# RWKV-style attention and a spatially gated block on one core: state and v of a head stacked to 128 rows from the second batch on

## The chip, the core and the metric

The kernel runs on one core of a Trainium2 chip. The metric is the device time of one execution in microseconds; for the kernel before, three runs gave a median of 352.72 us (351.6 to 352.75). One further execution was taken with the hardware profiler.

The engines are TensorE (PE in the profile; PEld is its weight loading), VectorE (DVE), ScalarE (ACT), GpSimd (POOL) and SyncE (SP), which here only issues DMA transfers. Each engine runs its own list of instructions in order and waits at semaphores.

## What is computed

Four batches, 8 heads, 768 tokens, head size 48; model width 384, inner width 1024, all float32.

```python
for t in range(S):                       # attention, state (B, H, 48, 48)
    cur = einsum('bhd,bhe->bhde', u * k[t], v[t])
    y[t] = einsum('bhd,bhde->bhe', r[t], state + cur)
    state = w[:, None] * state + einsum('bhd,bhe->bhde', k[t], v[t])
x = y as (B, S, 384)
h = maximum(x @ w_in, 0)                 # 384 -> 1024
u, v = h[..., :512], h[..., 512:]
v_n = (v - mean(v)) / sqrt(var(v) + 1e-6)
v_s = einsum('ts,bsd->btd', w_spatial, v_n) + b_spatial[None, :, None]
out = (u * v_s) @ w_out                  # 512 -> 384
```

## The kernel before

**Tiling.** Each batch is cut into 6 chunks of 128 tokens, so there are 24 chunks, numbered m. Tokens of a chunk lie in two halves of 64, z = 0 and 1, the first turned round, so that powers of the decay stay in range. The eight heads are four pairs p. For a chunk:

- `load_chunk` brings two tiles by SP's queue: `rk` (r and k with head dimensions on the partitions; 3 buffers) and `rkv` (r, k and v with tokens on the partitions; 3 buffers). v comes with each head's columns already padded with zeros to the width of a pair.
- `prep` multiplies rk by powers of the decay (on DVE and POOL for the first 7 chunks, on DVE alone after that), forms the diagonal term r * u * k summed over a head (three steps on `rkv`, a reduction to `dg`), scales k to `kn`, and writes the diagonal of the score tile `a`.
- `scores` multiplies k and r per head, 64x64, sixteen matmuls into PSUM tile `ps`.
- `products` multiplies k and v per head and half, sixteen matmuls of 64 stationary and 48 moving columns (eight in a batch's last chunk), into the other part of `ps`.
- `state` copies the masked scores into `a` (DVE), forms the state between the halves (`t`, "T1") and after the chunk (`s`), and lays each as blocks into a tile `sb` (ACT, two copies of 64x192 for each, function `block`).
- `apply` forms y transposed in PSUM tile `xp`: r times state, and scores times v. It is one group of matmuls with 32 stationary and 64 moving columns, 12 for each half that has a state and 24 for v: 48, or 36 in a batch's first chunk. Four column groups of 32 take turns.
- `fin` splits the result into a high part and a rest, tile `x`, both float32r, by a cast (ACT or DVE) and a subtraction on DVE.

The block after it works with pairs of such parts, three matmuls for each product (`mm3`: lines 556, 557, 558): `moe_v` (nine matmuls of 512 columns for a chunk), `moe_u` (nine of 384), `moe_sp` (eighteen of 384) and `moe_out` (twelve of 384). At the start `w_in`, `w_spatial` and `w_out` are turned into such pairs (`from_f64`, `split_sp`; three parts of w_in with matmuls at lines 367 to 369).

**The order.** A planner (`Plan.run`) builds the order of all five engines: every step is a task with the engines it may run on, a cost and a due time; at each step it takes, of the tasks that can start, the one that is late and due first, and books buffers. `pair`, `copy` and `relu` are steps with two possible engines. The order is then fixed; on the chip each engine runs its list.

Of the kernel before, what the change touches and what calls it, by code (L numbers as in the profile page):

```python
# [37 lines left out]
BIAS = 3  # L38
MOST_IN, MOST_OUT = 2, 1


class Task:
    def __init__(self, ways, lag, nominal, nbytes):
        self.ways, self.lag, self.nominal, self.nbytes = ways, lag, nominal, nbytes
        self.cost = min(w[1] for w in ways)
        self.before, self.after, self.bufs = set(), set(), []
        self.due = self.end = self.most = None
# [20 lines left out]
class Plan:  # L68
# [11 lines left out]
    def add(self, ways, r=(), w=(), lag=0.1, nominal=None, nbytes=0):  # L80
        t = Task(ways, lag, nominal, nbytes)
# [34 lines left out]

    CV = ("cv", "ws")
# [10 lines left out]

    def run(self):
        self.dues()  # L130
        left = {t: len(t.before) for t in self.tasks}
# [4 lines left out]
        while ready:  # L136
            best = {}
            for t in ready:
# [4 lines left out]
                if t.nbytes and len(landed) >= self.LANES:  # L143
                    can = max(can, landed[-self.LANES])
                end, e, at = min((max(can, free.get(e, 1.0)) + c + (BIAS if e == "DVE" else 0), e, max(can, free.get(e, 1.0)))
                                 for e, c, *_ in t.ways)
                late = at <= free.get(e, 1.0) + 0.02
                key = (0, t.due, t.place) if late else (1, at, t.due, t.place)
                if e not in best or key < best[e][0]:
                    best[e] = (key, at, t)  # L150
            if not best:
                raise ValueError(f"no slot for any of {len(ready)} ready tasks")
            _, at, t, e = min(((x[0], x[1], x[2], e) for e, x in best.items()), key=lambda x: (x[1], x[2].due))
# [31 lines left out]
            emit()  # L185
# [4 lines left out]
def fused_kernel(ctx, tc, rkT, rkvN, wT, uB, w_in, w_sp, b_sp, w_out, out):  # L190
# [4 lines left out]
    EARLY, STATS = 7, 1  # L195
# [3 lines left out]
    SLOTS = dict(rk=3, rkv=3, vn=6, gt=5, u=8, vs=4, g=2, ob=2, pm=4, ps=1, xp=1, x=2, s=2, t1=1, dg=2, q=2)  # L199
# [42 lines left out]
    def load(key, shape, dtype, src, nbytes, view=None, due=None):  # L242
# [3 lines left out]
        plan.add([("SP", 0.45, f, False)], (), [key], lag=0, nbytes=nbytes).most = due  # L246
# [11 lines left out]
    atiles = [const.tile([P, 2, 2, 2, HC], F32, name=f"a{n}") for n in range(2)]  # L258
    sblk = [const.tile([P, NP, 2 * D], F32, name=f"sb{n}") for n in range(2)]
# [10 lines left out]
    TMP = ("vs", "tmp")  # L270
# [4 lines left out]
    def sync(dst, src, key, nbytes, due=None):  # L275
        plan.add([("SP", 0.45, lambda: nc.sync.dma_start(out=dst, in_=src), False)], (), [key], lag=0,
                 nbytes=nbytes).most = due

    def setup():
# [36 lines left out]
        for n in range(2):  # L316
            pool(0, lambda n=n: nc.gpsimd.memset(sblk[n], 0.0), (), [("B", n)], cost=0.45)
# [20 lines left out]
    def load_chunk(m):  # L338
        b, c = divmod(m, NC)
        load(("rk", m), [P, 2, NP, C], F32, rkT[b, c], P * 2 * NP * C * 4)  # L340
        load(("rkv", m), [P, ROW], F32, rkvN[b, c], P * ROW * 4)
# [59 lines left out]
    def split_sp(j):  # L401
        K = ("gt", ("sp", j))
        for t in range(2):
# [3 lines left out]
            if (j, t) in SUM_SP:  # L407
# [6 lines left out]
                act(TH, lambda o=o, PS=PS: nc.scalar.copy(ws_l[:, j, o], T[PS][:, 0:TH]), [PS], [L])  # L414
# [6 lines left out]
    def prep(m):  # L421
        RK, RV, DG, A = ("rk", m), ("rkv", m), ("dg", m), ("A", m % 2)
        a = atiles[m % 2]
# [3 lines left out]
        if m < EARLY:  # L427
            pool(512, lambda: nc.gpsimd.tensor_tensor(out=rk()[:, 1], in0=rk()[:, 1], in1=tt, op=ALU.mult),
                 [RK, *TT], [k_], cost=1.1)
# [7 lines left out]
        pool(DM, lambda: nc.gpsimd.tensor_tensor(out=n_(), in0=n_(), in1=k0(), op=ALU.mult), [RV], [rn])  # L437
# [22 lines left out]
    def products(m):  # L460
        PS, RV = ("ps", m), ("rkv", m)

        def f():
            ps, rkv = tile_of(PS, [P, 2, 512]), T[RV]
            kn, v = rkv[:, OK:OK + DM + 16], rkv[:, OV:ROW].rearrange("s (z p e) -> s z p e", z=2, p=NP)
            for p2, z, s0, t0, j, b in QUAD:
                if z == 1 and m % NC == NC - 1:
                    continue
                hs, p, o = slice(64 * (j ^ b), 64 * (j ^ b) + 64), 2 * b + p2, 256 + (2 * z + p2) * D
                kc = (4 * b + 2 * p2 + z) * D  # L470
                nc.tensor.matmul(ps[64 * j:64 * j + 64, b, o:o + D], kn[hs, kc:kc + 64],  # L471
                                 v[hs, z, p, j * D:(j + 1) * D], start=True, stop=True, skip_group_check=True)

        pe(0.6 if m % NC < NC - 1 else 0.37, f, [RV + ("kn",), RV], [PS + ("k",)], nominal=(2 * m, 2))

    def block(dst, src):
        d4 = dst.rearrange("p (b q) e -> p b q e", b=2)
        nc.scalar.copy(d4[0:64, :, :, 0:D], src[0:64])
        nc.scalar.copy(d4[64:P, :, :, D:2 * D], src[64:P])

    def state(m):
        c, PS, S0, S1, T1 = m % NC, ("ps", m), ("s", m - 1), ("s", m), ("t1", m)
        part = lambda z: T[PS][:, :, 256 + z * 2 * D:256 + (z + 1) * 2 * D].rearrange("p b (q e) -> p b q e", q=2)
        sh = [P, 2, 2, D]
        dve(512, lambda: nc.vector.copy_predicated(  # L485
            out=atiles[m % 2].rearrange("s b q z t -> s (b q) (z t)"),
            mask=mask_u.rearrange("s z t -> s (z t)").unsqueeze(1).to_broadcast([P, 4, P]),
            data=T[PS][:, :, 0:256].rearrange("s b (q c) -> s b q c", q=2)),
            [PS + ("s",), ("c", "mask"), ("A", m % 2)], [("A", m % 2)], cost=0.63)
        k_ = PS + ("k",)  # L490
        if c == 0:
            act(0, lambda: block(sblk[1], part(0)), [k_], [("B", 1)], cost=0.62)
            dve(192, lambda: nc.vector.tensor_copy(out=tile_of(T1, sh), in_=part(0)), [k_], [T1])
        else:
            act(0, lambda: block(sblk[0], T[S0]), [S0], [("B", 0)], cost=0.72)
# [337 lines left out]
```

## Time and profile before

| | |
|---|---|
| runs shown, median | 352.72 us (351.6, 352.75, 352.72) |
| profiled execution | 352.11 us, span 350.4 us |
| busy in the span: PE, DVE, ACT, POOL | 329.4, 171.2, 148.6, 225.3 us |
| chain that ended last, PE's share | 88% |
| `xp`, all matmuls of apply, PE busy | 38.15 us |
| granted clock | 1.000 |

The span runs from the first to the last instruction; the execution's own time lies 1.7 us above it. An engine's busy time counts overlapping instructions once. In lists of instructions, "idle" is the time in which the engine stood still just before one, with the engine or the transfer that ended the wait behind an arrow. A float32 matmul leaves two records, so counts in the trace are twice those in the code.

### The profile page before, as it was taken

To read this page: it belongs to the slowest core of one execution; us is meant where nothing else is said; L and a number is where in the kernel's file an instruction comes from. 1 tells how busy PE (TensorE), PEld (TensorE's weight loads), DVE (VectorE), ACT (ScalarE), POOL (GpSimd) and SP (SyncE) were. 2 spreads that over 40 slices of the span, in tenths; PEclk is the share of its full clock that TensorE was granted. 3 is DMA by queue.
4 is the path that set the end of the run, shared out by engine and by line. 5 is a ranking of instruction groups with operands and counts; after the bars stand their busy time and mean duration, and the time that the engine had idled before them with its cause. 6 is when DMAs were issued, how large, how long until landed. Compare 5 with 4: busy or idle time off the path is not lost.

```text
span 350.4 us, 11537 instructions
## 1 busy us (share of the span) xinstructions
PE 329.4 (94%) x5092; PEld 302.1 (86%) x5092; DVE 171.2 (49%) x353; ACT 148.6 (42%) x334; POOL 225.3 (64%) x215
## 2 busy tenths in 40 slices
PE   2876999899999999999999999999999999999994
PEld 1454678799999899999999899999999899999993
DVE  5598964878634555554233664454233343011030
ACT  4237867772333384641323374640323363611121
POOL 4888989999858765587855767486855240436310
PEclk9999999999999999999999999999999999999999
DMA  7999457762061344442153144342050000010101
GB/s 236 421 408 341 160 177 249 250 227 89 0 199 44 134 153 153 146 129 101 22 199 115 40 152 153 144 137 96 19 203 2 2 2 2 22 47 0 45 24 67
DMA packets 13153, 44.78 MB, mean 128 GB/s; under 512 B 1584, under 2 KB 4784, under 8 KB 13104
## 3 DMA queue, kind: packets, MB, share of 16 engines
q1 hardware_dynamic: 13104, 44.05, 35.4%
q8 instruction: 40, 0.66, 0.8%
q14 instruction: 9, 0.07, 0.1%
HBM read 39.32 MB, written 4.72 MB: 126 GB/s over the span
## 4 chain that ended last, share of the span: by engine, by line
PE 88%; DVE 6%; DMA 2%; issue 2%; ACT 1%; SPq 0%; DVEq 0%; ACTq 0%
PE pm L556 24%; PE pm L557 23%; PE pm L558 23%; PE xp L516 9%; PE ps L455 4%; PE ps L471 3%; DMA vn<-w_in 1%; PE pm L367 1%; DVE a L485 1%; DVE pm L355 1%; DVE vn L357 1%; DVE pm L359 1%; DVE rk L430 1%; DMA out<-ob 1%; DVE wi_l L378 1%
## 5 line engine op out<-in xcount | busy, mean ns | idle before, releaser
L556 PE MATMUL pm<-ws_h,vn 128*128 128x384 f32 x192 | 65.2, 340 | 0.0
L558 PE MATMUL pm<-ws_h,vn 128*128 128x384 f32 x192 | 64.7, 337 | 0.0
L557 PE MATMUL pm<-ws_l,vn 128*128 128x384 f32 x192 | 64.5, 336 | 0.0
L682 DVE TENSOR_TENSOR g<-pm,bb 128x384 f32<-128x384 f32 x32 | 17.8, 556 | 66.6 <-PE pm L558 62.7
L437 POOL TENSOR_TENSOR rkv<-rkv 128x384 f32<-128x384 f32 x24 | 26.3, 1096 | 37.2 <-DMA rkv<-rkvN 37.2
L229 POOL TENSOR_TENSOR vn<-vs,vn 128x512 fp32r<-128x512 f32 x24 | 32.6, 1378 | 27.2 <-ACT vn L233 14.8
L233 ACT CAST gt<-g 128x384 fp32r<-128x384 f32 x32 | 16.4, 514 | 72.6 <-POOL g L229 66.4
L229 POOL TENSOR_TENSOR g<-g,u 128x384 f32<-128x384 f32 x30 | 31.4, 1047 | 19.1 <-DVE g L682 19.1
L434 DVE TENSOR_TENSOR rk<-rk,tt 128x1024 f32<-128x1024 f32 x17 | 29.5, 1734 | 25.9 <-DMA rk<-rkT 25.9
L229 POOL TENSOR_TENSOR gt<-g,gt 128x384 fp32r<-128x384 f32 x30 | 30.5, 1016 | 15.0 <-ACT gt L233 15.0
L556 PEld LDWEIGHTS pm<-ws_h,vn 128*128 128x128 f32 x192 | 36.0, 188 | 0.3
L557 PEld LDWEIGHTS pm<-ws_l,vn 128*128 128x128 f32 x192 | 36.1, 188 | 0.0
L558 PEld LDWEIGHTS pm<-ws_h,vn 128*128 128x128 f32 x192 | 36.0, 188 | 0.0
L556 PE MATMUL pm<-wo_h,gt 128*128 128x384 f32 x96 | 32.9, 342 | 0.0
L556 PE MATMUL pm<-x,wi_h 128*128 128x384 f32 x93 | 32.5, 349 | 0.0
L558 PE MATMUL pm<-wo_h,gt 128*128 128x384 f32 x96 | 32.4, 338 | 0.0
L557 PE MATMUL pm<-wo_l,gt 128*128 128x384 f32 x96 | 32.4, 338 | 0.0
L557 PE MATMUL pm<-x,wi_h 128*128 128x384 f32 x93 | 31.4, 338 | 0.9 <-issue 0.9
L442 POOL TENSOR_TENSOR a<-diag,dg 128x512 f32<-128x512 f32 x24 | 26.1, 1086 | 8.2 <-PE xp L516 4.9
L558 PE MATMUL pm<-x,wi_l 128*128 128x384 f32 x93 | 31.3, 337 | 0.0
L485 DVE COPY_PREDICATED a<-mask,ps 128x512 f32<-128x512 uint32 x24 | 18.0, 751 | 25.8 <-PE ps L471 22.5
L441 POOL TENSOR_TENSOR rkv<-rkv,tn 128x384 f32<-128x384 f32 x24 | 30.2, 1260 | 0.0
(119 smaller groups left out, 701.4 us busy)
## 6 DMA issues: line engine op xcount, KB each, us to landing
rkv<-rkvN SPq DMA_DIRECT2D x24, 776.0 KB, 4.6
rk<-rkT SPq DMA_DIRECT2D x24, 512.0 KB, 6.0
out<-ob SPq DMA_DIRECT2D x24, 192.0 KB, 1.9
vn<-w_in SPq DMA_DIRECT2D x6, 512.0 KB, 10.2
gt<-w_sp SPq DMA_DIRECT2D x6, 384.0 KB, 10.5
gt<-w_out SPq DMA_DIRECT2D x4, 384.0 KB, 3.8
bb<-b_sp SPq DMA_DIRECT2D x1, 384.0 KB, 9.3
ub<-uB SPq DMA_DIRECT2D x1, 192.0 KB, 7.3
```

The lines of the kernel that those rows point to most:

```text
L229: plan.add([(e, cost[e], lambda e=e: engine[e].tensor_tensor(**f()), True) for e in ways.split()], r, w)
L233: emit = dict(DVE=lambda: nc.vector.tensor_copy(**f()), ACT=lambda: nc.scalar.copy(f()["out"], f()["in_"]))
L434: dve(1024, lambda: nc.vector.tensor_tensor(out=rk(), in0=rk(), in1=tt.unsqueeze(1).to_broadcast([P, 2, NP, C]), op=ALU.mult), [RK, *TT], ...
L437: pool(DM, lambda: nc.gpsimd.tensor_tensor(out=n_(), in0=n_(), in1=k0(), op=ALU.mult), [RV], [rn])
L441: pool(DM, lambda: nc.gpsimd.tensor_tensor(out=k0(), in0=k0(), in1=tn_f, op=ALU.mult), [RV, rn, *TN], [kn])
L442: pool(512, lambda: nc.gpsimd.tensor_tensor(out=a.rearrange("s b q z t -> s (b q z) t"), in0=diag.unsqueeze(1).to_broadcast([P, H, HC]), i ...
L485: dve(512, lambda: nc.vector.copy_predicated(out=atiles[m % 2].rearrange("s b q z t -> s (b q) (z t)"), mask=mask_u.rearrange("s z t -> s ...
L516: nc.tensor.matmul(xp[32 * g:32 * g + 32, z, jt * HC:(jt + 1) * HC], lhsT, rhs, start=(z, g) not in began, stop=True, skip_group_check=Tru ...
L556: nc.tensor.matmul(o, lh, rh, start=first, stop=False)
L557: nc.tensor.matmul(o, lh, rl, start=False, stop=False)
L558: nc.tensor.matmul(o, ll, rh, start=False, stop=last)
L682: dve(384, lambda: nc.vector.tensor_tensor(out=g(), in0=T[PM][:, 0:TH], in1=bb[:, ts_], op=ALU.add), [PM, ("c", "bb")], [G])
```

## The change

From the second batch on (chunk 6, `FIRST_CHUNKS`), the state of a head and its v share a stationary operand: v takes the 64 rows of the head's half, the state 48 of the other 64 rows, in the tile `rkv` itself, where `v` now comes with 64 columns for each head, half and pair. Apply is then 8 groups of four matmuls, 32 in all, in first chunks too. The moving operand is a new tile `A` (2 buffers) with scores and r stacked in the same way. It is filled by `move`: four copies of r (64x256) and two of `a` (64x512) for a chunk, each a DMA on SP's queue, an ACT copy or a DVE copy, as the planner picks. The state goes into `rkv` by four ACT copies of 48x96 in place of two of 64x192. In the first six chunks apply keeps its 48 or 36 matmuls.

`products` takes 48 stationary columns in place of 64 in all chunks; the rows of PSUM between are set to zero once. The PSUM tile `ps` is fixed. `rk` has 2 buffers in place of 3; `a` is one buffer that is written whole (it was two, set to zero at the start). The loads of `rkv` are 1536 columns in the first six chunks and 1792 later, where they were 1552.

The planner gets biases by engine and by step (`LEAN`, `BIAS`, `LATE`), three steps of `prep` may go to DVE, and five seeds shake due times and biases of a share of the tasks.

```diff
+ROW_E, ROW = OV + 2 * NP * 2 * D, OV + 2 * 2 * NP * HC
+FIRST_CHUNKS = 6
-BIAS = 3
+LEAN = 4.0
+CALM, LATE = 80.0, dict(DVE=1.0, SP=1.0)
+SEEDS = (200055, 200068, 200448, 200760, 200881)
+BIAS = dict(DVE=3.0, ACT=3.5)
...
+    def shake(self):
+        for seed in SEEDS:
+            rnd = random.Random(seed)
+            share, size = rnd.choice((0.01, 0.03, 0.1, 0.3)), rnd.choice((1.0, 3.0, 8.0))
+            for t in self.tasks:
+                if rnd.random() < share:
+                    t.due += rnd.uniform(-size, size)
+                    for w in t.ways:
+                        w.lean += rnd.uniform(-size, size)
...
-    SLOTS = dict(rk=3, rkv=3, vn=6, ...
+    SLOTS = dict(rk=2, rkv=3, a=1, A=2, vn=6, ...
...
+        if m >= EC:
+            move(RK + ("r",), ("A", m), "r", [(64 * (1 - t), t, slice(2 * b, 2 * b + 2), 64 * (t ^ b))
+                                              for b in range(2) for t in range(2)],
+                 lambda p, h: rk()[h:h + 64, 0, p])
+
+    def move(src, dst, part, places, source):
+        for o, t, p, h in places:
+            n = (p.stop - p.start) * C
+            out = lambda o=o, t=t, p=p: tile_of(dst, [P, 2, NP, C])[o:o + 64, t, p]
+            plan.add([("SP", 0.45, lambda ...: nc.sync.dma_start(out=out(), in_=source(p, h)), False, 64 * n * 4),
+                      ("ACT", (n + 220) / 1200, lambda ...: nc.scalar.copy(out(), source(p, h))),
+                      ("DVE", n / 960 + 0.1, lambda ...: nc.vector.tensor_copy(out=out(), in_=source(p, h)),
+                       True, 0, LEAN)],
+                     [src], [dst + ((part, t, p.start),)], lag=0.1)
...
-                nc.tensor.matmul(ps[64 * j:64 * j + 64, b, o:o + D], kn[hs, kc:kc + 64],
-                                 v[hs, z, p, j * D:(j + 1) * D], start=True, stop=True, skip_group_check=True)
+                nc.tensor.matmul(ps[64 * j:64 * j + D, b, o:o + D], kn[hs, kc:kc + D],
+                                 ve[hs, h, z, p, slice(0, D) if m < EC else slice(16 * h, 16 * h + D)],
+                                 start=True, stop=True, skip_group_check=True)
...
+        for b in range(2):
+            for j in range(2):
+                h = j ^ b
+                o = 64 * (1 - h)
+                nc.scalar.copy(sv[o:o + D, h, z, 2 * b:2 * b + 2, 16 * h:16 * h + D], src[64 * j:64 * j + D, b])
...
+            sv = T[RV][:, OV:ROW].rearrange("s (h z p e) -> s h z p e", h=2, z=2, p=NP)
+            right = T["A", m]
             for z, s0, t0 in SUBS:
...
+                for j, h in ((0, 0), (1, 0), (1, 1), (2, 1)):
+                    for p in range(NP):
+                        mm(z, j, p, sv[:, h, z, p, 32 * (j - h):32 * (j - h) + 32], right[:, h, p, t0:t0 + 64])
```

The order moves with it. On PE, before, the scores, products and apply of chunk 2 stand together, behind the apply of chunk 1 and one matmul of the first moe_v:

```order
L516 MATMUL xp<-a_82,rkv 32x64 x24
L578 MATMUL pm<-wi_l,x 128x512
L455 MATMUL ps<-rk 64x64 x16
L471 MATMUL ps<-rkv 64x48 x16
L516 MATMUL xp<-rk,sb_83 32x64 x12
L516 MATMUL xp<-rk,sb_84 32x64 x12
L516 MATMUL xp<-a_81,rkv 32x64 x24
L556 MATMUL pm<-wi_h,x 128x512
```

The same place on PE now, from the end of chunk 0's moe_v (L659) on; L584 is apply, L523 products, L504 scores:

```order
L659 MATMUL pm<-wi_l,x 128x512 x3
L584 MATMUL xp<-rk,A 32x64 x24
L584 MATMUL xp<-a,rkv 32x64 x24
L523 MATMUL ps<-rkv 48x48 x16
L504 MATMUL ps<-rk 64x64 x16
L637 MATMUL pm<-wi_h,x 128x512
L638 MATMUL pm<-wi_l,x 128x512
L639 MATMUL pm<-wi_h,x 128x512
```

Nine matmuls of the second moe_v, of which the last three rows are the first three, now stand between the scores and the apply of chunk 2. A little earlier, the third conversion of w_in (L400 to L402, L367 to L369 before) has moved ahead of the first projection matmuls.

On ACT, at the first chunk of the second batch, before (L478 and L479 lay the state into `sb`):

```order
L594 ACTIVATE vs,q<-pm 128x512
L233 CAST x<-xp 128x2x3x64
L596 ACTIVATE q<-q 128x1
L478 COPY sb_84<-ps 64x4x48
L479 COPY sb_84<-ps 64x4x48
L597 ACTIVATE pm,q<-vs,q 128x512
```

And the same place on ACT now; L545 lays a state into `rkv`, L490 moves scores into `A`:

```order
L675 ACTIVATE vs,q<-pm 128x512
L677 ACTIVATE q<-q 128x1
L678 ACTIVATE pm,q<-vs,q 128x512
L545 COPY rkv<-ps 48x2x48 x4
L490 COPY A<-a 64x512 x2
L545 COPY rkv<-s 48x2x48 x4
```

The cast of x has gone to DVE, and ten copies stand where two did; the four moves of r for this chunk are on SP's queue.

On SP's queue, the loads for chunks 5 to 7, before:

```order
L245 DMA rkv_570<-rkvN 128x1552
L245 DMA rk_574<-rkT 128x1024
L245 DMA rkv_710<-rkvN 128x1552
L245 DMA rk_730<-rkT 128x1024
L245 DMA rkv_858<-rkvN 128x1552
L245 DMA rk_862<-rkT 128x1024
```

And now, from the rk of chunk 6 (885) to that of chunk 8 (1055):

```order
L277 DMA rk_885<-rkT 128x1024
L277 DMA rkv_896<-rkvL 128x1792
L489 DMA A_986<-rk_885 64x256 x4
L277 DMA rk_1013<-rkT 128x1024
L277 DMA rkv_1034<-rkvL 128x1792
L277 DMA rk_1055<-rkT 128x1024
```

Moves of r (L489) stand between the loads and wait for the multiply of `rk`; later in the list two moves of `a` stand there as well.

More of the change, by code (lines that the diff above doesn't have):

```diff
@@ L142, in run @@
                 can = max([1.0] + [b.end for b in t.before] + [min(self.slots[k[0]])[0] for k in takes])
[L143 to L146, printed above, removed]
+                found = None
+                for way in t.ways:
+                    e = way.engine
+                    at = max(can, free.get(e, 1.0))
+                    if way.nbytes and len(landed) >= self.LANES:
+                        at = max(at, landed[-self.LANES])
+                    end = (self.landing(line, at, way.nbytes) if way.nbytes else at + way.cost) + (way.lean if t.due < CALM else LATE.get(e, 0.0))
+                    if found is None or end < found[0]:
+                        found = (end, e, at, way)
+                _, e, at, way = found
                 late = at <= free.get(e, 1.0) + 0.02
@@ L157, in run @@
                 s.remove(min(s))
-            _, cost, emit, two = next(w for w in t.ways if w[0] == e)
-            if two and e == "DVE":
+            cost = way.cost
+            if way.two and e == "DVE":
                 cost += sum(max(0.0, min(y, at + cost) - max(x, at)) for x, y in shared[-3:])
-            if two and e == "POOL":
+            if way.two and e == "POOL":
                 shared.append((at, at + cost))
@@ L184, in run, with fused_kernel @@
                     ready.append(a)
-            emit()
+            way.emit()
         assert all(t.end is not None for t in self.tasks)
 @with_exitstack
-def fused_kernel(ctx, tc, rkT, rkvN, wT, uB, w_in, w_sp, b_sp, w_out, out):
+def fused_kernel(ctx, tc, rkT, rkvE, rkvL, wT, uB, w_in, w_sp, b_sp, w_out, out):
     nc = tc.nc
@@ L340, in load_chunk @@
         load(("rk", m), [P, 2, NP, C], F32, rkT[b, c], P * 2 * NP * C * 4)
[L341 removed]
+        n, src = (ROW_E, rkvE[m]) if m < EC else (ROW, rkvL[m - EC])
+        load(("rkv", m), [P, ROW], F32, src, P * n * 4, lambda t: t[:, 0:n])
     EYE, NEG = ("c", "eye"), ("c", "neg")
@@ L490, in state @@
+            [PS + ("s",), ("c", "mask"), ("a", m)], [("a", m)], cost=0.63)
+        if m >= EC:
+            move(("a", m), ("A", m), "a", [(64 * h, h, slice(0, NP), 64 * h) for h in range(2)],
+                 lambda p, h: T["a", m][h:h + 64].rearrange("s b q z t -> s (b q) (z t)"))
         k_ = PS + ("k",)
         if c == 0:
-            act(0, lambda: block(sblk[1], part(0)), [k_], [("B", 1)], cost=0.62)
+            act(0, lambda: block(m, 1, part(0)), [k_, RV], [B1], cost=0.62 if m < EC else 1.05)
@@ L739, in fused_kernel @@
         convert_in(k)
-    for n in range(2):
-        pool(0, lambda n=n: nc.gpsimd.memset(atiles[n], 0.0), (), [("A", n)], cost=0.52)
     for j in range(NS):
```

208 lines of the change are left out of this document (119 added, 89 removed).

## The prediction

> **What bounds the kernel now.** I read the page's busy times and chain first, then the busy time by stretches of the span, then the timeline of PE, DVE and ACT up to 64 us.
>
> ```profile
> PE 329.4 (94%) x5092; PEld 302.1 (86%) x5092; DVE 171.2 (49%) x353; ACT 148.6 (42%) x334; POOL 225.3 (64%) x215
> PE 88%; DVE 6%; DMA 2%; issue 2%; ACT 1%; SPq 0%; DVEq 0%; ACTq 0%
> ```
>
> ```profile
> 0.00:9.66 9.66, 1.79 (x32) 1.50 (x32) 6.09 (x13) 4.05 (x9) 3.95 (x18) 1.00 0.77 255
> 9.66:17.00 7.34, 6.84 (x72) 3.79 (x72) 3.69 (x6) 2.16 (x5) 7.18 (x8) 1.00 1.02 421
> 17.00:27.45 10.45, 7.82 (x174) 4.89 (x174) 9.94 (x20) 3.97 (x10) 8.51 (x9) 1.00 1.03 409
> 27.45:35.00 7.55, 5.01 (x232) 3.98 (x232) 6.32 (x14) 6.22 (x17) 6.61 (x7) 1.00 0.88 327
> 35.00:49.06 14.06, 12.69 (x260) 9.87 (x261) 12.14 (x31) 9.67 (x28) 12.76 (x14) 1.00 0.56 197
> 49.06:62.00 12.94, 12.09 (x337) 10.16 (x336) 6.78 (x12) 9.86 (x24) 12.94 (x12) 1.00 0.63 204
> 62.00:345.90 283.90, 283.12 (x3988) 267.95 (x3988) 126.22 (x264) 112.23 (x245) 173.34 (x153) 1.00 0.27 93
> 345.90:350.40 4.50, 0.00 (x0) 0.00 (x0) 0.00 (x0) 0.48 (x1) 0.00 (x0) 0.98 0.34 124
> ```
>
> The columns behind the length are PE, PEld, DVE, ACT, POOL, granted clock, DMA share and GB/s. There are two regimes. From 62 to 346 us PE works 283.12 of 283.90 us, so each microsecond of PE work removed there leaves the span, while DVE (126) and ACT (112) have more than half of the stretch free. Before 62 us PE idles, and from 17 to 27.45 us DVE is the full engine, 9.94 of 10.45 us. What the change does to the two regimes has to be worked out apart.
>
> **Term 1, apply.** A float32 matmul is recorded twice, so x96 is the 48 matmuls of a chunk with an incoming state, and x72 the 36 of a batch's first chunk.
>
> ```profile
> 131.77 1.48 PE xp L516 x96
> 142.88 1.14 PE xp L516 x72
> ```
>
> Twelve matmuls are 0.34 us: 28.3 ns each, and 0.12 us that doesn't go with the count. The 32 of the new form, same shapes (32 columns stationary, 64 moving), come to 1.03 us. Fifteen chunks with state go from 1.48 to 1.03 (6.75 us), three first chunks from 1.14 to 1.03 (0.33): -7.1 us. If all of the time went with the count they would take 0.99 and the gain be 7.8; less than 7.1 needs a larger fixed part than these rows have. The first six chunks keep their 252 matmuls.
>
> **Term 2, k x v with 48 stationary columns in place of 64.** No row has 48 of them. The nearest:
>
> ```profile
> 52.90 0.69 PE L455 MATMUL ps<-rk 64*64 64x64 f32 x32
> 53.41 0.40 PE L471 MATMUL ps<-rkv 64*64 64x48 f32 x16
> 53.74 0.44 PE L556 MATMUL pm<-x,wi_h 128*128 128x384 f32 x1
> 59.57 0.63 PE L471 MATMUL ps<-rkv 64*64 64x48 f32 x32
> 60.13 0.44 PE L556 MATMUL pm<-x,wi_h 128*128 128x384 f32 x1
> L471 PE MATMUL ps<-rkv 64*64 64x48 f32 x704 | 14.6, 217 | 0.7 <-DVE a L485 0.4 <-issue 0.3
> L471 PEld LDWEIGHTS ps<-rkv 64*64 64x64 f32 x704 | 12.7, 135 | 1.1 <-DVE a L485 0.7 <-issue 0.4
> L516 PEld LDWEIGHTS xp<-a,rkv 128*32 128x32 f32 x1152 | 18.3, 110 | 1.8 <-issue 1.4 <-DVE a L485 0.5
> ```
>
> From start to next start, 8 matmuls take 0.33 us and 16 take 0.56: 28.8 ns each, as much as apply's 28.3, although 48 columns move here and 64 there. So the moving side doesn't set it. Either the 64 stationary columns do (a load is 135 ns at 64 columns and 110 at 32), and 48 would save a quarter, 7.2 ns on 352 matmuls, 2.5 us; or about 28 ns is a floor, and nothing is saved. Nothing in the rows makes fewer columns dearer. I take 0.8, nearer the floor, since apply with half the stationary columns is no quicker. The Trainium skill, "TensorE: Matmul & The Clock Gate", section "Back-to-back issue gap", lists 1 to 64 moving columns at one price, an issue floor; the trace agrees that 48 and 64 cost the same (28.8 and 28.3 ns). By that rule alone this term would be 0, and the sum 0.8 us smaller.
>
> **Term 3, the start.** Where PE waits in the first 50 us:
>
> ```profile
> 19.95 0.50 PE L578 MATMUL pm<-wi_h,x 128*128 128x512 f32 x1 [0.90 <-ACT x L233]
> 20.86 0.51 PE L578 MATMUL pm<-wi_h,x 128*128 128x512 f32 x1 [0.41 <-DVE x L550]
> 27.08 0.85 PE L516 MATMUL xp<-rk,sb 128*32 128x64 f32 x21 [0.69 <-ACT sb L478]
> 29.84 0.27 PE L516 MATMUL xp<-a,rkv 128*32 128x64 f32 x2 [1.19 <-issue]
> 30.47 0.69 PE L455 MATMUL ps<-rk 64*64 64x64 f32 x32
> 33.22 0.85 PE L516 MATMUL xp<-rk,sb 128*32 128x64 f32 x21 [1.13 <-ACT sb L478]
> ...
> 55.42 0.39 PE L556 MATMUL pm<-wi_h,x 128*128 128x512 f32 x1
> 57.58 0.88 PE L516 MATMUL xp<-rk,sb 128*32 128x64 f32 x48
> 61.96 0.45 PE L557 MATMUL pm<-x,wi_h 128*128 128x384 f32 x1 [0.85 <-issue]
> ```
>
> The stretches from 17 to 62 us hold 7.4 us of idle PE (their length less PE's time), 1.19 and 0.85 of it "issue", which I count on no order to remove. The new order puts chunk 1's nine projection matmuls (2.16 us by the rows at 55.42 and 57.58) between the scores and apply of chunk 2, where 1.13 us was lost, and the third conversion's matmuls between apply and projection of chunk 0, where 0.90 + 0.41 was lost: 2.4 us covered. Of the other 2.9 us, in smaller waits such as the 0.69, I take a third, 0.9. Against that, the list of DVE up to the last w_in conversion grows by one memset, one rkv x ub, four casts of x and one of w_sp, less one multiply of rk: about 3.0 us on an engine with 3.7 us free from 17 to 49 us, where a cast before lay on ACT. I put 0.3 of it on PE's path. Two buffers of rk instead of three make chunk 2's load wait for apply 0, which ends near 19 us:
>
> ```profile
> rk<-rkT SPq DMA_DIRECT2D x24, 512.0 KB, 6.0
> gt<-w_sp SPq DMA_DIRECT2D x6, 384.0 KB, 10.5
> L428 POOL TENSOR_TENSOR rk<-rk,tt 128x512 f32<-128x512 f32 x7 | 9.0, 1286 | 0.0
> ```
>
> It lands between 25 and 29.5 us (6.0, or 10.5 behind the w_sp loads now ahead of it), plus the multiply 26.3 to 30.8; scores 2 stood at 30.47, so nothing is charged. Sum of the start: -2.4 - 0.9 + 0.3 = -3.0. Ends: -5.4 if all idle but the issue stalls goes, +0.6 if DVE's 3.0 us come wholly through and only the 2.4 are won.
>
> **Term 4, the new copies.** For 18 chunks there are 108 moves into A: 70 on ACT, 13 on DVE, 25 on SP's queue, and eight small state copies per chunk on ACT where four stood. Nearest prices:
>
> ```profile
> L478 ACT COPY sb<-t 64x192 f32<-64x192 f32 x20 | 7.0, 351 | 16.7 <-DVE t L496 16.7
> L233 ACT CAST vn<-vs 128x512 fp32r<-128x512 f32 x24 | 13.6, 613 | 0.0
> L500 DVE TENSOR_TENSOR ps<-ps,t 128x192 f32<-128x192 f32 x20 | 7.2, 359 | 0.1
> L493 DVE COPY t<-ps 128x192 f32<-128x192 f32 x4 | 1.4, 356 | 0.8 <-ACT sb L479 0.8
> L485 DVE COPY_PREDICATED a<-mask,ps 128x512 f32<-128x512 uint32 x24 | 18.0, 751 | 25.8 <-PE ps L471 22.5 <-ACT sb L479 2.2 <-PE ps L455 1.1
> ```
>
> A move of a at 0.61, one of r at about 0.45, a state copy at most 0.35: under 3.5 us of ACT per chunk of some 11 us (131.77 to 142.88 above), with ACT at 40%. PE work between scores and apply of a chunk covers them, except in one place: chunk 6, where only eighteen projection matmuls stand between products and apply, 3.8 us (1.68 and 2.16, by the starts at 53.74, 55.42 and 57.58). The chain in that gap is two DVE operations of 0.36, the predicated copy 0.75, two moves of a at 0.61 on ACT: 2.7 us, 3.3 if the four state copies delay ACT. It fits with handoffs to spare for little; I take +0.5 for this and other waits, ends 0 and +2.
>
> **Sum.** -7.1 - 0.8 - 3.0 + 0.5 = -10.4. The profiled execution took 352.11 us (span 350.4, 1.7 around it), so 341.7; the median shown, 352.72, is 0.6 above it, so 342.3. The last 4.5 us keep their instructions.
>
> **Rivals.**
> A. The start gives nothing: DVE, full there, pays for the casts, and scores 2 waits for rk. For it speaks 9.94 of 10.45; against it that the covered waits have DVE's or ACT's work on their far side, which now runs under matmuls. 352.7 - 7.1 - 0.8 + 0.5 = 345.3, up to 347.4 with the +2 of term 4.
> B. The start gives all, and 48 columns their quarter: 352.7 - 7.1 - 2.5 - 5.4 = 337.7 with no waits later; half-way from the forecast to it is 340. DVE's fullness speaks against the whole of it, the equal 28 ns against the quarter.
> C. Slower. SP's queue is in order, and moves of r and a wait in it for DVE's multiply and predicated copy; the next rk and rkv loads stand behind them, with one buffer of rk fewer.
>
> ```profile
> rkv<-rkvN SPq DMA_DIRECT2D x24, 776.0 KB, 4.6
> L434 DVE TENSOR_TENSOR rk<-rk,tt 128x1024 f32<-128x1024 f32 x17 | 29.5, 1734 | 25.9 <-DMA rk<-rkT 25.9
> L437 POOL TENSOR_TENSOR rkv<-rkv 128x384 f32<-128x384 f32 x24 | 26.3, 1096 | 37.2 <-DMA rkv<-rkvN 37.2
> ```
>
> DVE and POOL already wait for these loads (25.9 and 37.2 us in all) without PE noticing, and rkv grows by 15%. A load held past the chunk's cover costs PE 1:1. It decides at 0.58 us a chunk (10.4 / 18: no change) and is slower by over 0.5% from 0.68; at 1.0 us a chunk the time is 352.7 - 10.4 + 18 = 360. Against it: load 6.0 and multiply 1.73 are 7.7 us of an 11 us period, and only 25 of 108 moves are on SP.
>
> **Chances and range.** Forecast (339.5 to 344.5) 0.56, A 0.21, B 0.14, C 0.09. The range 338 to 347.8 holds the forecast, all of A and most of B; the forecast's own range is 339.5 to 344.5. About 0.5%, 1.8 us, is what this measurement can tell from no change. Faster: forecast, A and B, 0.90, and a little of C; no change, C near 0.58 us a chunk, 0.03; slower 0.07.
>
> **What would show it.** Term 1: xp groups of 64 records taking 1.03 us. Term 2: k x v starts 28.8 ns apart, or 21.6. Term 3: PE idle from 17 us to the steady stretch down from 7.4 to about 4.4 us, no wait of scores 2 on rk. Term 4: PE waits under 1 us before apply of chunk 6, and none later. The prediction is wrong if PE waits on ACT's moves or on loads in each chunk, or if DVE's stretch before 45 us gets longer than the waits it saves.

## The result and the profile after

| | before | after |
|---|---|---|
| median, runs beside each other | 352.58 us (4 runs) | 339.89 us (4 runs, 339.43 to 341.45) |
| ratio, with its 95% interval | | 0.9654 [0.9617, 0.9690] |
| profiled execution, span | 352.11, 350.4 us | 341.45, 339.7 us |
| busy: PE, DVE, ACT, POOL | 329.4, 171.2, 148.6, 225.3 | 319.3, 213.5, 176.2, 209.8 |

By the ratio the changed kernel is 12.2 us faster (0.0346 of 352.58); the medians differ by 12.7. Ratios, here and below, compare mean times and leave out executions that took over 1.5% longer than the fastest of the same kernel, while medians are over all. The forecast was 342.3, and 338 to 347.8 as a range. The two profiled executions differ by 10.7 us, and that is what the traces can be asked about. The page of after, its busy times and the shares of its chain:

```profile
PE 319.3 (94%) x4588; PEld 291.9 (86%) x4588; DVE 213.5 (63%) x417; ACT 176.2 (52%) x438; POOL 209.8 (62%) x195
PE 83%; DMA 6%; POOL 4%; DVE 3%; issue 2%; SPq 1%; ACT 0%; DVEq 0%; ACTq 0%
```

PE lost 504 records (16 matmuls in each of 15 chunks and 4 in each of three first chunks, recorded twice) and 10.1 us of busy time; DVE and ACT gained 42 and 28 us. The chain now crosses transfers (6%, 2% before) and POOL (4%), a sign that there is less spare room round PE than there was.

Where the 10.7 us lie is read from the busy times by stretches, cut at 17 us by the clock and after that at the same work in both traces: at the start of apply 6 (the first stacked one), at the end of apply 23, at PE's end. Columns: stretch, length, then PE, PEld, DVE, ACT and POOL busy, granted clock, DMA share, GB/s. Before:

```profile
0.00:17.00 17.00, 8.63 (x104) 5.28 (x104) 9.77 (x18) 6.22 (x14) 11.13 (x25) 1.00 0.88 327
17.00:65.17 48.17, 40.78 (x1018) 31.41 (x1022) 38.03 (x79) 32.79 (x84) 43.99 (x42) 1.00 0.74 269
65.17:290.98 225.81, 225.50 (x3670) 211.69 (x3669) 113.40 (x233) 94.64 (x207) 154.24 (x135) 1.00 0.31 108
290.98:345.42 54.44, 54.44 (x310) 53.74 (x306) 9.96 (x24) 14.48 (x29) 15.94 (x15) 1.00 0.06 23
345.42:350.40 4.98, 0.00 (x1) 0.00 (x0) 0.00 (x0) 0.51 (x2) 0.00 (x0) 0.98 0.32 118
```

After:

```profile
0.00:17.00 17.00, 8.81 (x176) 5.79 (x176) 13.33 (x25) 7.17 (x15) 10.55 (x22) 1.00 0.87 328
17.00:62.70 45.70, 38.93 (x942) 30.20 (x942) 38.48 (x81) 27.19 (x71) 40.11 (x38) 0.96 0.69 249
62.70:282.20 219.50, 217.58 (x3166) 202.55 (x3165) 148.60 (x285) 127.95 (x325) 143.99 (x122) 1.00 0.41 137
282.20:336.22 54.02, 54.02 (x307) 53.35 (x306) 13.05 (x28) 13.39 (x27) 15.16 (x14) 1.00 0.09 30
336.22:339.70 3.48, 0.00 (x0) 0.00 (x0) 0.00 (x0) 0.48 (x1) 0.00 (x0) 0.97 0.16 57
```

Up to apply 6: 2.5 us won. From there to the end of apply 23: 6.3. To PE's end: 0.4. Behind PE: 1.5. In the long stretch PE's busy time fell by 7.9 (225.50 to 217.58), and its idle time rose from 0.3 to 1.9.

The rows of PE that answer to the terms: k x v of a last and of a full chunk, each with the next row, and apply 6.

```profile
50.51 0.36 PE L523 MATMUL ps<-rkv 64*48 64x48 f32 x16
50.79 0.44 PE L637 MATMUL pm<-x,wi_h 128*128 128x384 f32 x1
58.39 0.54 PE L523 MATMUL ps<-rkv 64*48 64x48 f32 x32
58.86 0.44 PE L637 MATMUL pm<-x,wi_h 128*128 128x384 f32 x1
62.71 1.13 PE L584 MATMUL xp<-A,rkv 128*32 128x64 f32 x64
63.76 0.44 PE L637 MATMUL pm<-x,wi_h 128*128 128x384 f32 x1
```

Start to start, eight k x v matmuls take 0.28 us and sixteen 0.47: 23.75 ns each, where 28.8 stood (the rows are given to 0.01 us, so this is good to some 2 ns). Apply takes 1.05 from start to start. And PE's waits of over 0.75 us from 20 us on, with what ended them:

```profile
22.71 0.57 PE L523 MATMUL ps<-rkv 64*48 64x48 f32 x32 [1.96 <-DVE a L552]
28.64 0.98 PE L504 MATMUL ps<-rk 64*64 64x64 f32 x32 [1.28 <-POOL rk L462]
...
53.57 0.47 PE L637 MATMUL pm<-wi_h,x 128*128 128x512 f32 x1 [0.95 <-DVE x L265]
66.38 0.69 PE L504 MATMUL ps<-rk 64*64 64x64 f32 x32 [0.76 <-DVE rk L468]
75.58 1.15 PE L584 MATMUL xp<-A,rkv 128*32 128x64 f32 x64 [1.16 <-issue]
```

The last two are new in kind. The scores of chunk 7 wait for DVE's multiply of rk, and DVE had itself stood 2.80 us for the load of that rk:

```profile
65.10 1.23 DVE L468 TENSOR_TENSOR rk<-rk,tt 128x1024 f32<-128x1024 f32 x1 [2.80 <-DMA rk<-rkT]
```

Apply 7 waits for something that the profile does not name. After 76 us PE doesn't wait for as long as 0.3 us in one place.

### The profile page after: what moved, and what is told of

Its sections match the earlier page's. It is cut to its first block, busy times and chain, and to the rows that moved or that the text cites. A ratio compares the mean times of both kernels' runs of the same rounds, so it can differ in the third digit from the quotient of the medians.

```text
span 339.7 us, 10768 instructions
## 1 busy us (share of the span) xinstructions
PE 319.3 (94%) x4588; PEld 291.9 (86%) x4588; DVE 213.5 (63%) x417; ACT 176.2 (52%) x438; POOL 209.8 (62%) x195
## 4 chain that ended last, share of the span: by engine, by line
PE 83%; DMA 6%; POOL 4%; DVE 3%; issue 2%; SPq 1%; ACT 0%; DVEq 0%; ACTq 0%
PE pm L637 25%; PE pm L639 23%; PE pm L638 23%; PE xp L584 6%; PE ps L504 4%; DMA rk<-rkT 3%; DMA vn<-w_in 3%; PE ps L523 2%; POOL rkv L260 1%; POOL rk L462 1%; SPq L277 1%; POOL vn L260 1%; POOL a L260 1%; DVE pm L388 1%; PE pm L659 0%
## 5 line engine op out<-in xcount | busy, mean ns | idle before, releaser
L260 POOL TENSOR_TENSOR a<-diag,dg 128x512 f32<-128x512 f32 x24 | 27.0, 1126 | 38.5 <-ACT A L490 15.2
L265 ACT CAST gt<-g 128x384 fp32r<-128x384 f32 x28 | 14.2, 513 | 60.7 <-POOL g L260 51.3
L260 POOL TENSOR_TENSOR gt<-g,gt 128x384 fp32r<-128x384 f32 x28 | 29.8, 1067 | 17.1 <-ACT gt L265 16.2
L260 POOL TENSOR_TENSOR g<-g,u 128x384 f32<-128x384 f32 x27 | 29.5, 1093 | 15.3 <-DVE g L763 15.1
L468 DVE TENSOR_TENSOR rk<-rk,tt 128x1024 f32<-128x1024 f32 x17 | 28.9, 1699 | 11.2 <-DMA rk<-rkT 9.8
L260 POOL TENSOR_TENSOR vn<-vs,vn 128x512 fp32r<-128x512 f32 x16 | 22.9, 1444 | 21.1 <-ACT vn L265 21.1
L260 POOL TENSOR_TENSOR rkv<-rkv,tn 128x384 f32<-128x384 f32 x24 | 31.2, 1298 | 1.5 <-DVE rkv L260 1.5
L260 POOL TENSOR_TENSOR rkv<-rkv 128x384 f32<-128x384 f32 x21 | 22.0, 1049 | 15.1 <-DMA rkv<-rkvL 9.2
L637 PE MATMUL pm<-wi_h,x 128*128 128x512 f32 x69 | 28.0, 406 | 0.9 <-DVE x L265 0.9
## 6 DMA issues: line engine op xcount, KB each, us to landing
vn<-w_in SPq DMA_DIRECT2D x6, 512.0 KB, 10.1
gt<-w_sp SPq DMA_DIRECT2D x6, 384.0 KB, 10.2
```

Source lines behind the costliest of these rows:

```text
L265: emit = dict(DVE=lambda: nc.vector.tensor_copy(**f()), ACT=lambda: nc.scalar.copy(f()["out"], f()["in_"]))
L468: dve(1024, lambda: nc.vector.tensor_tensor(out=rk(), in0=rk(), in1=tt.unsqueeze(1).to_broadcast([P, 2, NP, C]), op=ALU.mult), [RK, *TT], ...
L637: nc.tensor.matmul(o, lh, rh, start=first, stop=False)
```

## Experiments

Two things were open: how much each part of the change is worth by itself, and whether the order, which the forecast took as given and priced only by its waits, is itself what the time hangs on. Times below are medians; ratios are against the kernel before, run beside.

**Stationary columns alone.** The kernel before with 48 stationary columns in k x v, a fixed `ps` tile and its zeroes; nothing else.

```diff
-                nc.tensor.matmul(ps[64 * j:64 * j + 64, b, o:o + D], kn[hs, kc:kc + 64],
+                nc.tensor.matmul(ps[64 * j:64 * j + D, b, o:o + D], kn[hs, kc:kc + D],
```

> The kernel before, with k x v on 48 stationary columns in place of 64 and nothing else (PSUM tile fixed, its spare rows set to zero once; order of all engines kept). In the changed kernel a set of 16 products went from 0.56 to 0.47 us, start to next start, a set of 8 from 0.33 to 0.28. Theory, the stationary columns set the time: 20 x 0.09 + 4 x 0.05 = 2.0 us off, 350.6 us. Rival, a floor of 28 ns per matmul, the shorter sets being due to what stands behind them: no change, 352.6.

350.52 us, ratio 0.9951 [0.9936, 0.9966]: 1.7 us faster. Fewer stationary columns make these matmuls quicker, so 28 ns was no floor: the trace's own slope, (28.8 - 23.75) ns on 16 or 8 matmuls of 24 chunks, is 20 x 0.08 + 4 x 0.04, some 1.8 us. The Trainium skill, "TensorE: Matmul & The Clock Gate", section "Back-to-back issue gap", lists one price for 1 to 64 moving columns, and by that alone this would be 0; the same section says that weight loading and matmul set the spacing together, which is the half that the runs bear out (a load is 122 ns at 48 columns, 135 at 64).

**No seeds.** The changed kernel with `SEEDS = ()`: same instructions for PE, another order.

> The changed kernel with an empty list of seeds, so due times aren't shaken; stacking, 48 columns, biases and buffers stay. PE's work is the same. Theory, the gain is PE's work (7.1 apply + 2.0 products) and the rest, about 3.6 us, is the order of the start and the end, half of it from the seeds: 341.5 us. Rival 1, the seeds carry all that goes beyond PE's work: 343.5 or more. Rival 2, they do nothing on the chip: 339.9.

352.19 us, ratio 0.9983 [0.9956, 1.0009], from 349.24 to 357.61 in twelve runs. The number lies in rival 1's open range, "343.5 or more", but rival 1 kept the gain of PE's work, and that is gone too: without the five seeds nothing is left of the gain that this measurement can tell from no change. PE has the same matmuls in it as the kernel that takes 339.9. In the two profiles PE's busy time is 321.3 us here and 319.3 there, and its idle time in the span 27.2 and 20.4.

**No seeds and no stacking.** All 24 chunks in the first form.

```diff
-FIRST_CHUNKS = 6
+FIRST_CHUNKS = 24
-SEEDS = (200055, 200068, 200448, 200760, 200881)
+SEEDS = ()
```

> The changed kernel without stacking (FIRST_CHUNKS = 24) and without seeds: apply keeps 48 or 36 matmuls in all chunks, no moves into A. To be held against the run without seeds. Theory, apply's count is worth 15 x 0.45 + 3 x 0.11 = 7.1 us and its copies are hidden: 7 us above the run without seeds, about 348.5. Rival, the copies and waits for loads take a part back in the changed kernel: only 4 to 5 us above it, with fewer waits of PE here than there.

353.59 us, ratio 1.0044 [1.0017, 1.0070]. Between this and the run above stacking is worth 1.4 us by the medians and 2.1 by the ratios, not 7.1. In the stretch from apply 6 to apply 23 the two profiles, this one first, say why:

```profile
65.20:291.80 226.60, 223.61 (x3670) 209.46 (x3669) 141.40 (x278) 82.27 (x184) 125.90 (x117) 1.00 0.32 112
65.00:289.70 224.70, 218.94 (x3166) 204.12 (x3165) 154.01 (x292) 122.78 (x309) 143.93 (x125) 0.99 0.39 129
```

PE's work falls by 4.7 us, at a lower clock, and its idle time rises from 3.0 to 5.8, while ACT has 40 us more to do.

**Other seeds, and the planner as it was.** First `SEEDS = (1, 2, 3, 4, 5)`, then the stacked kernel with the settings of before:

```diff
-LEAN = 4.0
-CALM, LATE = 80.0, dict(DVE=1.0, SP=1.0)
-SEEDS = (200055, 200068, 200448, 200760, 200881)
-BIAS = dict(DVE=3.0, ACT=3.5)
+LEAN = 99.0
+CALM, LATE = 1e9, {}
+SEEDS = ()
+BIAS = dict(DVE=3.0)
```

> SEEDS = (1, 2, 3, 4, 5) in place of the five in the change: a shake that nobody chose by its time. Theory (it is this one order that is quick, the shake as such gives nothing): 349 to 356, like the orders without seeds (352.2 and 353.6). Rival (any spreading of the due times takes the waits away): 339 to 345.

> Stacked chunks and 48 columns as in the change, but the planner's settings of before: no seeds, LEAN 99 (so that DVE isn't offered the new ways), the bias of 3 for DVE alone, CALM never reached. Theory (without a chosen order the copies' waits take back most of apply's 7 us): 349 to 354. Rival (the new leans and biases are what hurts without the seeds, the old ones keep the 7 + 2 us): 343 to 346.

357.82 us, ratio 1.0156 [1.0130, 1.0181], and 360.34 us, ratio 1.0250 [1.0210, 1.0289]. A shake as such gives nothing, and both came out slower than their theories had it. With the old settings the stacked kernel, 9 us lighter on PE, is 8.4 us slower than before. Much of the cost lies in one place, the stretch from 60 to 90 us, where the first stacked chunks, the conversion of w_out and the loads meet. Old settings, then the changed kernel:

```profile
60.00:90.00 30.00, 21.31 (x413) 17.95 (x412) 20.75 (x41) 23.10 (x64) 22.16 (x18) 0.84 0.35 118
60.00:90.00 30.00, 28.08 (x385) 26.07 (x385) 23.80 (x47) 16.67 (x45) 27.90 (x25) 1.00 0.76 257
```

PE stands for 8.7 us of the 30 and the mean granted clock is 0.84; in the changed kernel it stands for 1.9 at the full clock.

**Which part of the order.** The same draws of the same five seeds, but put to use only on tasks due before 62 us, or only on the others:

```diff
+        plain = {t: t.due for t in self.tasks}
...
+                    on = float(plain[t] < 62.0)
-                    t.due += rnd.uniform(-size, size)
+                    t.due += on * rnd.uniform(-size, size)
...
-                        w.lean += rnd.uniform(-size, size)
+                        w.lean += on * rnd.uniform(-size, size)
```

> The five seeds draw the same numbers as in the changed kernel, but only the due times and leans of tasks due before 62 us are shaken. The no-seeds run, 352.2, and the changed kernel, 339.9, differ by 12.3 us; in the profiled executions 2.3 of it lie before apply of chunk 6, 5.2 between there and the end of apply 23, 1.3 behind the last matmul. Theory (the stretches add up, each stretch keeps what its own order gives): the start's 2.3 are won, 349.5 to 350.5. Rival (the start's order sets how far the copies are ahead of PE from then on, so that the late shake only follows): 342 to 345. Rival (an order holds as a whole only): 352.

> The same draws, but only tasks due at 62 us or later are shaken; PE's list then differs from the changed kernel's by about 100 lines, nearly all in the start. Theory (stretches add up): the steady part and the tail come out as in the changed kernel, the start as without seeds: 341.5 to 345, with a start of apply 6 at 65 us and from there to the end of apply 23 219.5 to 221 us. Rival (the start decides): 349 to 352, with 223 us or more in that stretch.

Early alone: 344.80 us, ratio 0.9801 [0.9759, 0.9842], which is in the first rival's range. Late alone (`>=`): 347.92 us, ratio 0.9880 [0.9827, 0.9934], between its theory and its rival. The two gains against the run without seeds are 7.4 and 4.3 us by the medians and 6.4 and 3.6 by the ratios; both shakes together give 12.3 and 11.6. With intervals of 1 to 2 us on each, the time adds up by parts, but not by the parts in which I had put it. Long stretch and tail, early alone:

```profile
61.80:283.40 221.60, 217.21 (x3166) 202.47 (x3165) 154.31 (x295) 126.29 (x318) 142.58 (x122) 1.00 0.39 135
337.44:342.30 4.86, 0.00 (x0) 0.00 (x0) 0.00 (x0) 0.51 (x2) 0.00 (x0) 0.94 0.34 121
```

and late alone:

```profile
65.30:289.20 223.90, 219.21 (x3166) 204.31 (x3165) 148.00 (x286) 125.80 (x318) 143.55 (x121) 0.98 0.39 131
343.20:346.50 3.30, 0.00 (x0) 0.00 (x0) 0.00 (x0) 0.48 (x1) 0.00 (x0) 1.00 0.16 60
```

Against 65.0, 224.7 and 4.8 without seeds, the early shake wins 3.2 us before apply 6 and 3.1 behind it, and nothing of the tail; the late one wins the tail's 1.5. The early one's 3.1 fit the rival's mechanism, that the start decides how the stacked chunks meet the loads; no run here singles it out. What is left to the late one in the long stretch is seen at apply 13. Early alone, then the changed kernel:

```profile
148.64 0.54 PE L523 MATMUL ps<-rkv 64*48 64x48 f32 x32
150.52 1.10 PE L584 MATMUL xp<-A,rkv 128*32 128x64 f32 x64 [1.34 <-DVE x L631]
```

```profile
149.54 0.69 PE L504 MATMUL ps<-rk 64*64 64x64 f32 x32
150.17 0.45 PE L637 MATMUL pm<-ws_h,vn 128*128 128x384 f32 x1
...
153.50 1.10 PE L584 MATMUL xp<-A,rkv 128*32 128x64 f32 x64
```

In the first, apply 13 follows the scores and products at once and stands for 1.34 us until DVE has read the `xp` of the chunk before (one buffer); in the second, matmuls of moe_sp lie between the scores and apply 13, and the same DVE step is waited for by nobody.

**What "issue" before apply 7 is.** Late alone has one large wait left, 4.69 us before apply 7, put down to "issue"; the changed kernel has 1.16 there. In both, transfers of chunk 7's `a` into `A` are under way on SP's queue: in late alone they are issued from 73.50 us on and take 7.1 us at the median to land, and apply 7 starts at 80.89. The edit turns these two moves, and nothing else, into ACT copies, in the changed kernel and in late alone; every instruction of PE, DVE and POOL keeps its place.

```diff
-("SP", 0.45, lambda ...: nc.sync.dma_start(out=out(), in_=source(p, h)), ...
+("SP", 0.45, lambda ...: nc.scalar.copy(out(), source(p, h)) if src == ("a", 7) else nc.sync.dma_start(...), ...
```

> The changed kernel with one edit: the two moves of chunk 7's a into tile A are copies on ACT instead of transfers on SP's queue; every other instruction keeps its place. In the changed kernel PE waits 1.16 us before apply 7, put down to issue, while a transfer of a that was issued at 70.4 us is under way. Theory (the landing of that transfer ends the wait; two copies of 0.62 us on ACT are done by 72 us): the wait goes, the time falls by 1.0 to 1.6 us, to 338.3 to 338.9. Rival (issue is PE's own affair, and ACT, 1.24 us later with its next operations, delays something else): 339.9 to 341.5, and the wait before apply 7 stays.

> The same edit in the kernel whose start isn't shaken (late shake only, 347.9). There PE waits 4.69 us before apply 7, and apply 7 then takes 1.93 us instead of 1.03, scores 8 1.06 instead of 0.62. Theory: the wait and the slow rows behind it go, 6 us in all: 341.5 to 342.5. Theory with the wait alone (slow rows have another cause): 343.2. Rival (issue is PE's own): 347 to 349.

Late alone goes to 343.46 us, ratio 0.9768 [0.9717, 0.9818], 4.5 less by the medians and 3.9 by the ratios: about the wait's own length, and short of the 6 us that the first theory had. In its profile the long stretch is 218.60 us, 5.3 shorter, with a new wait of 1.36 us before scores 8; its start came out 4 us longer in that one execution, which ran for 13.6 us before apply 6 at half the clock, where the profile without the edit has 6.8, and waited 2.0 us before a part of apply 4 where that one waited 0.4. The changed kernel goes to 339.66, ratio 0.9643 [0.9613, 0.9674], which can't be told from 339.89: the wait went, as its theory had it, and the time did not. Late alone without the edit and with it, then the changed kernel with it:

```profile
80.89 1.93 PE L584 MATMUL xp<-A,rkv 128*32 128x64 f32 x64 [4.69 <-issue]
80.06 1.10 PE L584 MATMUL xp<-A,rkv 128*32 128x64 f32 x64
```

```profile
74.05 1.10 PE L584 MATMUL xp<-A,rkv 128*32 128x64 f32 x64
78.89 0.44 PE L639 MATMUL pm<-ws_h,vn 128*128 128x384 f32 x1 [0.62 <-POOL vn L260]
```

The wait is gone in both, so "issue" there was the landing of the transfer. Not every "issue" is one: late alone also has 3.03 us of it before a matmul of moe_v (at 26.87 us), which does not read `A`. Where most of the saving goes in the changed kernel is seen in the last row: 5 us later PE waits 0.62 us for a `vn` that POOL has not finished, and apply 8 begins 18.8 us after apply 7 where it was 17.9. From apply 6 to apply 8 the two profiles differ by 0.4 us (30.37 and 30.73).

**Copies doubled.** Each ACT copy of a move or a state is issued twice, in the same order.

```diff
-                nc.scalar.copy(sv[o:o + D, h, z, 2 * b:2 * b + 2, 16 * h:16 * h + D], src[64 * j:64 * j + D, b])
+                for _ in range(2): nc.scalar.copy(sv[o:o + D, ...], src[64 * j:64 * j + D, b])
```

> The changed kernel with each ACT copy of the moves and of the state blocks from chunk 6 on issued twice: about 69 us more of ACT (33.5 for moves, 35.2 for state copies), order of all engines kept. Theory, the copies lie under PE's matmuls: at most a wait before apply of chunk 6, where 3.8 us cover a chain of 2.7 to 3.3 us that grows by up to 2.2 us: 340 to 342 us. Rival, the copies are near the path in each chunk: 18 chunks x 0.5 us or more, 349 us and up.

369.31 us, ratio 1.0490 [1.0462, 1.0517]: ACT's busy time rises by 66.5 us (to 242.7) and the kernel by 29. PE's waits in it:

```profile
PE xp L584 <- DVE x L631: 7.0, 2, 4.0
PE pm L637 <- DVE q L708: 4.6, 1, 4.6
PE xp L584 <- ACT A L490: 2.6, 3, 1.3
```

The copies are covered in the changed kernel, but not by much: twice the work on an engine that is 52% busy comes through at 0.44 us for each us. Between the two profiles (366.5 and 339.7 us) PE's idle time grows by 18.8 us and its busy time by 8.0, with the same matmuls: 17 us of this run are at half the clock, 3.4 in the changed kernel. Of PE's two largest waits the first is for a DVE step that takes what ACT has made (L631 stands 12.5 us for ACT's cast of `x`).

**PE's work put back.** The changed kernel with 48 matmuls in the stacked apply: those of the middle column group are issued twice.

```diff
                         mm(z, j, p, sv[...], right[:, h, p, t0:t0 + 64])
+                        if j == 1: mm(z, j, p, sv[...], right[:, h, p, t0:t0 + 64])
```

> The changed kernel with the PE work of apply put back: in the 18 stacked chunks the 16 matmuls of the middle column group are issued twice, 48 in place of 32, at the same place and with the same copies (the second adds its product once more to xp). Theory (apply's matmuls are worth their time 1:1 in this order): 18 x 16 x 28.3 ns = 8.2 us more, 347.5 to 348.7. Rival (part of PE's time is slack under the copies): 343 to 346.

352.00 us, ratio 0.9972 [0.9944, 1.0001]: 12.1 us more, where 1:1 would be 8.2. So PE's time has no slack under the copies; in this order the stacked apply is worth all of its matmuls, and the shift of the rest costs on top. Of its profile's 12.6 us in the long stretch (232.10 against 219.50), 8.2 are the matmuls by the estimate above, 1.2 the longer wait before apply 7 (2.32 for 1.16), 1.4 a new one at 256 us, and about 1.7 the clock behind the first: 2.1 us at 0.61 and 3.0 at 0.70.

## Why the prediction was right, and where it was wrong

The forecast's number held, and the order's own account was nearly its steps': -10.4 forecast, -10.7 in the profiled executions. But three terms were mis-sized and one was missing. That the errors cancel is luck:

| | forecast | measured |
|---|---|---|
| 1, apply | -7.1 | -7.1 by its rows; in this order worth at least that (work put back) |
| 2, k x v with 48 columns | -0.8 | -1.7 alone, -1.8 by its rows |
| 3, the start | -3.0 | -2.5 up to apply 6, 0.5 of it from term 2: -2.0 |
| 4, copies and new waits | +0.5 | about +2.1 |
| behind PE and just ahead of its end | 0 | -1.9 |

Term 4 is what is left over: the long stretch is 6.3 us shorter, where apply gives 7.1 and k x v 1.3 (17 of the 24 chunks).

Term 1 stood as worked out: 1.05 us from start to start, for 1.03.

Term 2 failed at the step "nearer the floor, since apply with half the stationary columns is no quicker". Apply loads its 32 columns over all 128 rows and k x v its 64 over 64, and the comparison across shapes did not hold. For the same reason the equal 28.8 and 28.3 ns could not show that the moving columns are free: the two differ in their stationary shape as well. The other end that was named, a quarter, was 2.5; 1.7 came.

Term 3's size was nearly right, its mechanism less so. Idle time of PE from 17 us on was to fall from 7.4 to about 4.4 us; it fell to 6.8 (45.70 less 38.93). The waits named did go, the 1.13 before apply of chunk 2 and the 0.90 + 0.41 on the casts. But products 1 now wait 1.96 us for the predicated copy, and scores 2 wait 1.28 for rk 2: rival A's wait, which the prediction had costed at nothing. The rest of the start's gain is shorter PE time. Part of that is chance. The second pair of conversion matmuls, before, after, and in the run with chunk 7's moves on ACT, whose PE list is that of the changed kernel:

```profile
12.39 1.91 PE L367 MATMUL pm<-vn,eye 128*128 128x512 f32 x2
11.65 1.14 PE L400 MATMUL pm<-vn,eye 128*128 128x512 f32 x2
11.74 1.91 PE L400 MATMUL pm<-vn,eye 128*128 128x512 f32 x2
```

So the quick pair belongs to the one execution and not to the change. The start's gain did not hang on it: the other run begins apply 6 at 62.44 us, for 62.70.

Term 4 was +2.1, just above the end of its range, and in another place: no wait before apply 6, which was the one named, but 0.76 before scores 7 and 1.16 before apply 7. The first is rival C's mechanism, a load of rk that comes too late for DVE's multiply, at one chunk instead of all 18. The second is a neighbour of it: there loads stood behind moves, here a move of `a` lands late. Rival A's upper end, 347.4, was added up wrongly: with +2 in place of +0.5 for term 4 it is 346.8. The range to 347.8 holds both.

The tail was taken as unchanged because its instructions are. ACT's last copy, before and after, shows what moved:

```profile
346.94 0.48 ACT L233 COPY ob<-pm 128x384 f32<-128x384 f32 x1 [1.48 <-DMA out<-ob]
336.30 0.48 ACT L265 COPY ob<-pm 128x384 f32<-128x384 f32 x1 [1.62 <-PE pm L639]
```

Before, it waited for an earlier output to leave its buffer; now only for PE. By the two half-shaken kernels the late shake carries this (tails of 4.86 and 3.30 us).

What the prediction did not see is how narrow its ground was. It read the waits of one order and priced the copies as covered, "ends 0 and +2". That was true of this order alone: the same matmuls and the same pieces copied took 352.2, 357.8 and 360.3 us in three other orders of the same planner, and 344.8 and 347.9 with half of the shake. Rival C's point of no change, 10.4 us given back, was reached or passed in the first three, if by more kinds of waits than the one it named. Nor are waits all of it: in the profiles of these three PE's idle time is 27.2, 30.3 and 32.1 us, for 20.4 in the changed kernel, and its busy time, for the same matmuls, 321.3, 325.6 and 325.9, for 319.3. The surplus of busy time is about what half the clock costs there: 8.5, 14.8 and 17.6 us of PE's work ran at 0.50, for 3.4 in the changed kernel. The part of the planner that looked like noise, five seeds, carries 12.3 us by the medians and 11.6 by the ratios, as much as the whole gain: the 9 us of PE work that the change removes come through only in an order that covers the copies. The order alone could not have done it either, since the kernel before had only 0.3 us of idle PE in its long stretch. Half settled is why the kernel without seeds scatters over 8 us with one and the same order: its quickest run, 349.24 us, has a mean granted clock of 0.985 and its longest, 357.61, one of 0.972, and 0.013 of 350 us would be at most 4.6 of the 8.4, as an estimate. What makes the clock fall in one execution and not in the next is open. An order chosen by seeds for the unstacked form was not tried.

## What to carry to other kernels

When a change takes work off the engine that bounds the kernel and puts more onto its neighbours, price the work from rows, but then ask how many microseconds of cover each new step has, since that, not the share of busy time, says whether the gain stays. Test it with the order changed and the work kept: if the time moves by as much as the gain, the order is part of the change. Where a wait is put down to "issue" and a transfer into the waiting tile is in flight, replace the transfer by a copy before looking for another cause.

## What the runs showed of the hardware

A wait of PE can cost more than its own length. Granted clock in late alone, behind the 4.69 us wait:

```profile
80.80:83.00 2.20, 2.11 (x72) 1.97 (x76) 1.35 (x1) 0.12 (x1) 2.09 (x2) 0.50 0.06 22
83.00:85.00 2.00, 2.00 (x66) 1.91 (x63) 0.41 (x2) 1.46 (x6) 1.92 (x3) 0.50 0.51 119
```

Up to 85.7 us, for 4.8 us behind the wait, the clock is 0.50, and the 64 matmul records of apply take 1.93 us instead of 1.10: some 2.4 us more in all, as an estimate from the clock. Without seeds, a wait of 2.14 us before apply 7 is followed by three microseconds at 0.56, and one of 1.73 us later in that run by 1.00:

```profile
80.00:83.00 3.00, 3.00 (x77) 2.88 (x70) 1.19 (x3) 2.50 (x9) 3.00 (x3) 0.56 0.82 262
234.50:238.00 3.50, 3.47 (x78) 3.41 (x79) 3.33 (x8) 2.74 (x9) 1.04 (x1) 1.00 0.82 250
```

The Trainium skill, "TensorE: Matmul & The Clock Gate", section "HAM oscillation — how this bites in real kernels", advises against gaps of more than about 3.4 us. Here single gaps of 2.14 and 2.32 us already brought the clock down. But the length alone does not decide. The wait of products 1 is of one length in the changed kernel and in the run with chunk 7's moves on ACT:

```profile
22.71 0.57 PE L523 MATMUL ps<-rkv 64*48 64x48 f32 x32 [1.96 <-DVE a L552]
24.90 0.61 PE L523 MATMUL ps<-rkv 64*48 64x48 f32 x32 [1.95 <-DVE a L552]
```

In the second the clock is 0.50 from 25.3 to 28.7 us, and at 1.00 again behind the 1.25 us before scores 2. In the first it stays at 1.00 and falls only behind the 1.28 us before scores 2, to 0.50 from 28.9 to 32.3. With the seeds 1 to 5, 2.15 us of waiting (at 47.13 us) leave it at 1.00.

What does repeat is the length of the fall. The kernel before has none in its profile; the twelve others have 24 that end before PE's last matmul, and each of them, added up from windows of a quarter of a microsecond, amounts to 3.4, 6.8 or 10.2 us at 0.50. With PE at work all through, the shortest costs 1.7 us, as an estimate: nearly as much again as the 1.95 us of waiting ahead of it.

The clock column does not tell of the first microseconds. It reads 1.00 up to 17 us before and after the change, while the pair of conversion matmuls above takes 1.91 us in one and 1.14 in the other, and the next pair 1.14 in both.

How soon a transfer between tiles lands differs much: over the whole changed kernel a move of 128 KB lands in 4.5 us at the median, and between 68 and 78 us, beside loads of rkv, rk and w_out, in 5.0; in late alone between 68 and 82 us, beside the same kinds of loads, in 7.1. That the other transfers make the difference is likely but not shown. An ACT copy of the same piece takes 0.62 us.

```profile
A<-a SPq DMA_DIRECT2D x6, 128.0 KB, 4.5
A<-a SPq DMA_DIRECT2D x2, 128.0 KB, 7.1
L490 ACT COPY A<-a 64x512 f32<-64x512 f32 x24 | 14.9, 619 | 8.4 <-DVE a L552 8.2
```
